# Copying x of the last two attention steps out of each PSUM bank with one ScalarE operation of 512 columns in place of two of 256

## The chip, the cores and the metric

The kernel runs on one core of a Trainium2 chip. The core's engines work side by side and each takes its own instructions in order: TensorE (PE for its matmuls, PEld for its weight loads), VectorE (DVE), ScalarE (ACT), GpSimd (POOL) and SyncE (SP), which issues most DMAs. Matmuls write into PSUM, eight banks of 512 f32 columns in 128 partitions; the other engines copy results from there to the on-chip memory SBUF. The metric is the device time of one execution in microseconds (us), the median of the runs shown.

## What is computed

A linear attention with decay, followed by a two-layer network with a tanh gelu. There are 4 batches, 8 heads, 768 positions, head width 64; the network goes from 512 to 2048 and back to 512 columns for 3072 tokens.

```python
for b in range(nb):                       # blocks of 64 positions
    intra = (q_b @ k_b^T * Dmask) @ v_b   # within the block, lam ** distance below the diagonal
    inter = (q_b * lam_pow) @ kv_state    # from all earlier blocks
    out[b] = intra + inter
    kv_state = lam**64 * kv_state + (k_b * rev_pow)^T @ v_b
x = out as 3072 tokens x 512              # 8 heads side by side
h = x @ w_in                              # 512 -> 2048
g = 0.5 * h * (1 + tanh(c * (h + 0.044715 * h**3)))
return g @ w_out                          # 2048 -> 512
```

## The kernel before

**Attention by steps.** The attention runs in 24 steps. A step is 256 positions of one batch (a "super-block", numbered 0 to 11) and one half of the heads, so steps 2n and 2n + 1 make up super-block n. For a step, q and k are scaled, cast and transposed; `scores` multiplies k with q into two banks S; `causal` (L360) multiplies the scores with the mask into PT on VectorE; PT and v give the part of x within the chunks of 128 positions (L460), and the running state u with q gives the rest (L498, or L488 for some steps, called narrow, whose second chunk lands in the other half of the partitions). Both are summed in PSUM in the two banks O0 and O1, one for each chunk of 128 positions; a step takes 256 columns of each bank. The state is advanced by `update` (VectorE L547 and L550, GpSimd L558 and L565).

**Two steps at once.** `burst(ns, ss, ...)` runs the scores of the steps `ns` and finishes x of two steps `ss`, which fill the two halves of both banks. It then makes the masked scores of `ns` (`causal`), copies x out of the banks, queues the network's work for the finished group of super-blocks, and advances the states of `ns`. Five bursts come before the last call, `burst((), (22, 23), 3, 4)`: here no scores are left to make, so `ns` is empty, and 22 and 23 are not narrow.

**Copying x.** `x_out(ss, O, swapped)` copies x of the steps in `ss` from the banks to the f16 tile xT of the group: for each of the banks c = 0, 1 one ScalarE operation (L529), or for the second bank of narrow steps two operations of 64 partitions each (L527). Each pair of neighbouring output columns comes from two places 64 columns apart in the bank, so the copy writes f16 values with a stride of two. For narrow steps, the two steps of a burst are given to `x_out` together (512 columns per operation); for other steps, one after the other (256 columns per operation). Four operations thus run in the last burst, in this order: step 22 from O0, step 22 from O1, step 23 from O0, step 23 from O1.

**The network by groups.** The network works on groups of super-blocks; the last group, number 6, holds super-blocks 10 and 11, that is steps 20 to 23. For groups 5 and 6 the first product, x times w_in, is made by a scheme of seven block products in place of eight (`seven`, matmuls at L796 into banks HX, HY and HW). It needs sums and differences of quarters of x, made by `sum_x` on VectorE (L775, tile xs). The quarters are numbered (C, T): C is the half of the columns (the head half), T the super-block within the group:

```python
X_SUMS = {1: ((0, 1), ALU.subtract, (0, 0)), 2: ((1, 1), ALU.subtract, 1),
          3: ((1, 1), ALU.subtract, (0, 1)), 4: ((1, 0), ALU.subtract, 2)}
```

So the first sum reads the quarter (0, 1), which is step 22, and the second reads the first sum and the quarter (1, 1), step 23. The block products of a set come in the order 1, 5, 2, 6, 3, 7, 4, where 4 falls into the next set. Product 1 (into HX) reads the quarter (0, 0) alone, which is step 20; product 5 (into HY) reads the first sum; product 2 (into HW) reads the quarter (1, 0); product 6 (HX) reads the second sum; product 3 (HY) reads the quarter (1, 1). ScalarE copies HX (L808, tile m) and HY (L808, tile q) for later additions on VectorE (L818), and writes the gelu (L814). The second layer is made by seven products too (`product`, matmuls at L692 into banks MX, MY and MW, copies at L714, additions at L734, L740 and L743).

**What sets the order.** The order of every engine's instructions is written out by hand: each one is pinned in program order. The network's pieces stand in a list `filler`, and calls of `fill(n)` between the attention's steps take n pieces from it. After the last burst, `fill(len(filler))` takes all that are left: first the rest of group 5's second layer, with group 6's products between them. The first piece taken after the last burst is a product MY of group 5, and the four `sum_x` of group 6 are issued behind it; on VectorE they stand behind an addition of group 5 (L734) that was issued before. SyncE's and GpSimd's queues hold nothing between the last states (L565) and the output's stores and an addition (L749) of group 5.

The profile names lines of the kernel: L498 matmuls that finish x, L529 the copies, L775 the sums of x, L796 the first layer's products of groups 5 and 6, L692 the second layer's.

Of the kernel before, what the change touches and what calls it, by code (L numbers as in the profile page):

```python
# [15 lines left out]
def kernel(  # L16
# [322 lines left out]
    def half64(i):  # L339
        return slice(64 * i, 64 * i + 64)  # L340
# [3 lines left out]
    def scores(n):  # L344
        o = qkT[n]
        Sps = [ps_M.tile([P, 2, 2, P], FP32, tag="M", name=f"S{hl}") for hl in range(2)]
        for hp in range(2):
            for jk in range(2):
                for hl, c in TILES:
                    pin(nc.tensor.matmul(  # L350
                        Sps[hl][half64(c), hp, jk, :], o[half64(hl), 1, jk, hp, half64(c)],
                        o[half64(hl), 0, :, hp, half64(c)], start=True, stop=True,
                        skip_group_check=True))
        Ss[n] = Sps

    def causal(n):

        t = ptp.tile([P, 2, 2, 2, P], FP16, tag="PT", name=f"PT_{n}")
        for hl, Sps in enumerate(Ss.pop(n)):
            pin(nc.vector.tensor_tensor(  # L360
                t[:, hl].rearrange("p b c d -> p b (c d)"), Sps[:].rearrange("p b c d -> p b (c d)"),
                mask[:].unsqueeze(1).to_broadcast([P, 2, 2 * P]), ALU.mult))
        PTs[n] = t
# [65 lines left out]
    def behind(ins):  # L429


        nop = nc.tensor.nop()
        tc.add_manual_dep(nop.ins, ins.ins.name, mybir.DependencyInfo(
            mybir.DependencyClass.Sync, mybir.DependencyReason.DATA))
        pin(nop)

    def burst(ns, ss, *mix, ahead=None):


        narrow = bool(NARROW & set(ss))  # L440
        for i, n in enumerate(ns):
            scores(n)
            if ahead and i == 0:
                ahead()
        O = [ps_M.tile([P, 2, 2, P], FP32, tag="M", name=f"O{c}") for c in range(2)]
        seen = set()

        def start(kind, c, hl):
            new = (kind, c, hl) not in seen
            seen.add((kind, c, hl))  # L450
            return new

        qTs = [qkT.pop(s) for s in ss]
        for i, s in enumerate(ss):
            PT, tv = PTs.pop(s), a16.pop(s)[2]
            for hp in range(2):
                for jk in range(2):
                    for c, hl in TILES:
                        to = hl ^ narrow * c
                        mm = nc.tensor.matmul(  # L460
                            O[c][half64(to), i, hp, :], tv[half64(c), jk, 2 * hp + hl, :],
                            PT[half64(c), hl, hp, jk, :], start=start("O", c, to), stop=False,
                            skip_group_check=True)
                        pin(mm)
        if ns:
            K = [ps_M.tile([P, 2, P], FP32, tag="M", name=f"K{c}") for c in range(2)]
        for i, n in enumerate(ns):
            _, tk, tv = a16[n]
            last = (n // 2) % NSB == NSB - 1
            for jk in range(2):  # L470
                for hp in range(2):
                    for c, hl in TILES:
                        if c == 1 and last:
                            continue
                        pin(nc.tensor.matmul(
                            K[c][half64(hl), i, hp * D : hp * D + D],
                            tk[half64(c), jk, 2 * hp + hl, :], tv[half64(c), jk, 2 * hp + hl, :],
                            start=start("K", c, hl), stop=(jk == 1), skip_group_check=True))
            Kps[n] = [t[:, i] for t in K]
        if narrow:  # L480
            behind(mm)
        for i, s in enumerate(ss) if narrow else ():
            u = [us.pop(key, None) for key in ((s - 2, 1), (s, 0))]
            for hp in range(2):
                for c, hl in TILES:
                    if u[c] is None:
                        continue
                    pin(nc.tensor.matmul(  # L488
                        O[c][half64(hl ^ c), i, hp, :], u[c][half64(hl), hp, :],
                        qTs[i][half64(hl), 0, :, hp, half64(c)], start=False, stop=True,  # L490
                        skip_group_check=True))
        for i, s in enumerate(ss) if not narrow else ():
            for c in range(2):
                if c == 0 and (s // 2) % NSB == 0:
                    continue
                u = us.pop((s, 0) if c else (s - 2, 1))
                for hp in range(2):
                    pin(nc.tensor.matmul(O[c][:, i, hp, :], u[:, hp].rearrange("p l d -> p (l d)"),  # L498
                                         qTs[i][:, 0, :, hp, half64(c)], start=False, stop=True,
                                         skip_group_check=True))  # L500
        for n in ns:
            causal(n)
        for batch in ((ss,) if narrow else [(s,) for s in ss]):
            i = ss.index(batch[0])
            x_out(batch, [t[:, i : i + len(batch)].rearrange("p i h t -> p (i h t)") for t in O],
                  swapped=narrow)
        sbg = ss[-1] // 2
        g, i = group_of[sbg]
        if ss[-1] % 2 == 1 and i == len(groups[g]) - 1:
            queue_group(g, *mix)  # L510
        for n in ns:
            update(n, 0)

    def x_out(ss, O, swapped=False):

        sbg, half = divmod(ss[0], 2)
        g, i = group_of[sbg]
        if g not in xT:
            xT[g] = xtp.tile([P, len(groups[g]), 2, 2, SB], FP16, tag="xT", name=f"xT_{g}")
        r = 4 * i + 2 * half  # L520
        dst = xT[g].rearrange("p b a h t -> p (b a h) t")[:, r : r + 2 * len(ss)]
        for c in range(2):
            d = dst[:, :, c * P : (c + 1) * P].rearrange("p r (t j) -> p r j t", j=2)
            o = O[c].rearrange("p (r j t) -> p r j t", j=2, t=D)
            if c == 1 and swapped:
                for hl in range(2):
                    pin(nc.scalar.activation(out=d[half64(hl)], in_=o[half64(1 - hl)], func=AF.Copy))  # L527
            else:
                pin(nc.scalar.activation(out=d, in_=o, func=AF.Copy))  # L529
# [5 lines left out]
    def update(s, c, parts="tu"):  # L535


        sbg, half = divmod(s, 2)
        sb = sbg % NSB
        if c == 1 and sb == NSB - 1:  # L540
            Kps.pop(s)
            return
        if "t" in parts:
            K = (Kps[s] if c == 0 else Kps.pop(s))[c].rearrange("p (hp d) -> p hp d", hp=2)
            t = ucp.tile([P, 2, D], FP32, tag=f"t{half}", name=f"t_{s}_{c}")
            if sb == 0 and c == 0:
                pin(nc.vector.tensor_copy(out=t[:], in_=K))  # L547
            else:
                for hp in range(2):
                    pin(nc.vector.scalar_tensor_tensor(  # L550
                        t[:, hp, :], state[half][:, hp, :],
                        lamu[:, 2 * half + hp : 2 * half + hp + 1], K[:, hp, :],
                        ALU.mult, ALU.add))
            state[half] = t
        if "u" in parts:
            if (s if c == 0 else s + 2) in NARROW:
                u = ubp.tile([P, 2, 2, D], FP16, tag=f"u{half}", name=f"u_{s}_{c}")[:, 0]
                pin(nc.gpsimd.tensor_tensor(  # L558
                    u, state[half][:],
                    lamu[:, 2 * half : 2 * half + 2].unsqueeze(2).to_broadcast([P, 2, D]),  # L560
                    ALU.mult))
                us[(s, c)] = u
                return
            u = ubp.tile([P, 2, 2, D], FP16, tag=f"u{half}", name=f"u_{s}_{c}")
            pin(nc.gpsimd.tensor_tensor(  # L565
                u[:], state[half][:].unsqueeze(2).to_broadcast([P, 2, 2, D]),
                lumask[:, 2 * half : 2 * half + 2, :].unsqueeze(3).to_broadcast([P, 2, 2, D]),
                ALU.mult))
            us[(s, c)] = u
# [566 lines left out]
    scale_v(16)  # L1136
    fill(3)
    burst((13, 14), (12,))
    fill(1)
    U(13)  # L1140
# [30 lines left out]
    fill(3)  # L1171

    burst((18, 19), (16, 17))
    prep_v(21)
    fill(2)
# [49 lines left out]
```

## Time and profile before

| | |
|---|---|
| median of 3 runs | 198.75 us (198.57 to 198.77) |
| the profiled execution's own time | 198.57 us |
| its span, first to last instruction | 196.8 us |
| granted TensorE clock, mean | 0.997 |
| TensorE matmul busy | 189.8 us, 96% of the span |
| VectorE busy | 145.8 us, 74% |
| ScalarE busy | 126.0 us, 64% |
| copies of x from O (L529) | 13: 10 of 128x256, 3 of 128x512 |
| last burst's copies | 159.52 to 160.91 us |
| last instruction of the chain | ScalarE copy L714, 192.95 to 193.33 us |

A line of the profile has the start and the length in us, the engine, the source line, the operation, the tiles (written<-read), the size of the operands (partitions x elements, type) and the number of such operations run together; behind it, in brackets, the idle time of the engine before it and what ended it. In the groups the last columns are the busy time and the mean length in ns. The chain of work that ended last is followed back from the last instruction: at each step to what released it, or to the instruction before it on its engine. Times are counted from the start of the span.

### The profile page before, as it was taken

Reading aid. Unit: us, or ns where it says so; the run is one execution under the profiler, and the core shown is the slowest. Engines: PE = TensorE matmul, PEld = TensorE weight load, DVE = VectorE, ACT = ScalarE, POOL = GpSimd, SP = SyncE. Lnnn points to the kernel's source line nnn. Section 1 sums busy time; section 2 is a strip of 40 time slices with the busy share of each in tenths; the row PEclk is TensorE's granted clock in tenths of the full one; section 3 lists DMA queues with packets and bytes.
Section 4 is the critical chain, followed back from the end, with each engine's and each line's share of the span. In section 5 each row is a group of like instructions: output and inputs, shape, how many; then the busy total and the mean of one; then the engine's idle time right before and its main releaser. Section 6 shows DMA issues by size and latency. Waiting matters only on the chain.

```text
span 196.8 us, 5996 instructions
## 1 busy us (share of the span) xinstructions
PE 189.8 (96%) x2467; PEld 138.7 (70%) x2469; DVE 145.8 (74%) x291; ACT 126.0 (64%) x250; POOL 68.9 (35%) x85
## 2 busy tenths in 40 slices
PE   8879999999999999999999999999999999999992
PEld 2546544456888888654688754588888888888881
DVE  4987722889999789959989836999557995478530
ACT  3673878357874796686846479835778856678211
POOL 6594213456445524438434506064002030002000
PEclk9999999999999999999999999999999999999998
DMA  5999999999999999999989999910630300021114
GB/s 171 291 324 384 388 384 389 299 289 291 242 217 218 250 215 238 240 176 267 331 253 236 269 344 154 152 27 0 47 113 3 110 5 0 3 107 67 43 61 154
DMA packets 62811, 38.13 MB, mean 194 GB/s; under 512 B 18624, under 2 KB 55744, under 8 KB 62784
## 3 DMA queue, kind: packets, MB, share of 16 engines
q1 hardware_dynamic: 62240, 37.50, 78.8%
q8 instruction: 19, 0.31, 0.7%
q10 hardware_dynamic: 544, 0.26, 0.5%
q14 instruction: 8, 0.07, 0.1%
HBM read 27.26 MB, written 6.29 MB: 171 GB/s over the span
## 4 chain that ended last, share of the span: by engine, by line
PE 89%; SPq 4%; DMA 4%; ACT 0%; issue 0%
PE Hps L613 25%; PE MX L692 18%; PE MY L692 9%; PE HX L796 7%; PE O2ps L628 7%; PE MW L692 4%; DMA wi<-in_moe_w_in_dram 4%; SPq L70 4%; PE HY L796 4%; PE S L350 3%; PE Hps L895 3%; PE HW L796 2%; PE O L460 1%; PE OK L400 1%; PE Tps L321 1%; PE OK L422 1%
## 5 line engine op out<-in xcount | busy, mean ns | idle before, releaser
L613 PE MATMUL Hps<-xT,w_in 128*128 128x512 f16 (+1 forms) x288 | 50.5, 332 | 0.0
L613 PEld LDWEIGHTS <-w_in 128*128 128x128 f16 x288 | 27.8, 98 | 19.4
L617 ACT ACTIVATE gT<-Hps 128x512 f16<-128x512 f32 x56 | 32.6, 597 | 9.0 <-PE Hps L613 8.5
L360 DVE TENSOR_TENSOR PT<-S,mask 128x512 f16<-128x512 f32 x48 | 30.4, 683 | 8.9 <-PE S L350 8.9
L266 POOL TENSOR_TENSOR v<-v,dv 128x512 f16<-128x512 f32 x24 | 27.7, 1156 | 19.4 <-DMA v<-in_v_dram 14.5
L692 PEld LDWEIGHTS <-gs 128*128 128x128 f16 x320 | 31.1, 98 | 3.7
L692 PEld LDWEIGHTS <-gT 128*128 128x128 f16 x240 | 23.2, 98 | 3.5 <-ACT gT L617 0.2
L565 POOL TENSOR_TENSOR u<-t,lumask 128x256 f16<-128x256 f32 x21 | 15.6, 757 | 21.1 <-DVE t L550 11.9
L692 PE MATMUL MX<-w_sum,gs 128*128 128x256 f16 x160 | 21.4, 273 | 0.0
L282 DVE TENSOR_TENSOR qk<-q,dq 128x512 f16<-128x512 f32 x23 | 19.0, 830 | 0.7 <-DMA q<-in_q_dram 0.5
L295 ACT ACTIVATE qk<-k 128x512 f16<-128x512 f32 x23 | 14.4, 625 | 7.8 <-DMA k<-in_k_dram 7.2
L749 POOL TENSOR_TENSOR o<-u,q 128x512 f32<-128x512 f32 (+1 forms) x5 | 6.0, 1197 | 37.2 <-issue 34.7
L662 DVE TENSOR_TENSOR gs<-gT 128x1024 f16<-128x1024 f16 (+1 forms) x24 | 16.1, 678 | 3.1 <-ACT gT L617 3.0
L558 POOL TENSOR_TENSOR u<-t,lamu 128x128 f16<-128x128 f32 x19 | 10.9, 582 | 19.7 <-DVE t L550 14.1
L628 PE MATMUL O2ps<-w_out,gT 128*128 128x512 f16 x64 | 14.6, 379 | 0.0
L796 PEld LDWEIGHTS <-ws 128*128 128x128 f16 x128 | 12.4, 98 | 1.6 <-DVE xs L775 0.2
L529 ACT ACTIVATE xT<-OK 128x256 f16<-128x256 f32 x22 | 8.7, 453 | 6.4 <-PE OK L413 3.1
L714 ACT ACTIVATE u<-MX 128x256 f32<-128x256 f32 x18 | 6.9, 384 | 7.4 <-PE MX L692 7.4
L628 PEld LDWEIGHTS <-gT 128*128 128x128 f16 x64 | 6.1, 98 | 6.6
L692 PE MATMUL MY<-w_out,gs 128*128 128x256 f16 x80 | 10.7, 273 | 0.0
L810 DVE COPY u<-HX 128x512 f32<-128x512 f32 x8 | 5.5, 690 | 6.8 <-ACT gT L814 4.4
L692 PE MATMUL MX<-w_sum,gT 128*128 128x256 f16 x80 | 10.4, 273 | 0.0
(105 smaller groups left out, 322.5 us busy)
## 6 DMA issues: line engine op xcount, KB each, us to landing
q<-in_q_dram SPq DMA_DIRECT2D x24, 256.0 KB, 5.2
k<-in_k_dram SPq DMA_DIRECT2D x24, 256.0 KB, 5.5
v<-in_v_dram SPq DMA_DIRECT2D x23, 256.0 KB, 5.4
out_dram<-o SPq DMA_DIRECT2D x23, 256.0 KB, 3.7
wo<-in_moe_w_out_dram SPq DMA_DIRECT2D x4, 1024.0 KB, 9.4
wi<-in_moe_w_in_dram SPq DMA_DIRECT2D x4, 512.0 KB, 7.2
wi<-in_moe_w_in_dram SPq DMA_DIRECT2D x2, 1024.0 KB, 12.6
v<-in_v_dram ACTq DMA_DIRECT2D x1, 256.0 KB, 4.2
```

The source lines that it names most:

```text
L266: pin(nc.gpsimd.tensor_tensor(wide(tv[:]), ld32[s][2][:], decay(dv, s), ALU.mult))
L282: pin(q_eng.tensor_tensor(wide(tq), q32[:], decay(dq, s), ALU.mult))
L295: pin(nc.scalar.activation(out=wide(tk), in_=k32[:], func=AF.Copy))
L360: pin(nc.vector.tensor_tensor(t[:, hl].rearrange("p b c d -> p b (c d)"), Sps[:].rearrange("p b c d -> p b (c d)"), mask[:].unsqueeze(1).t ...
L558: pin(nc.gpsimd.tensor_tensor(u, state[half][:], lamu[:, 2 * half : 2 * half + 2].unsqueeze(2).to_broadcast([P, 2, D]), ALU.mult))
L565: pin(nc.gpsimd.tensor_tensor(u[:], state[half][:].unsqueeze(2).to_broadcast([P, 2, 2, D]), lumask[:, 2 * half : 2 * half + 2, :].unsqueez ...
L613: pin(nc.tensor.matmul(by_block(Hps[:, i, :]), w_in16[:, c, f * P : (f + 1) * P], x(c), start=(c == 0), stop=(c == NC - 1)))
L617: pin(nc.scalar.activation(out=dst, in_=Hps[:], func=AF.Gelu_apprx_tanh))
L628: pin(nc.tensor.matmul(O2[tau][0][:], gT[:, f % HF, f // HF, tau * P : (tau + 1) * P], w_out16[:, f, :], start=(n == 0), stop=(n == NF - 1)))
L662: pin(nc.vector.tensor_tensor(g_rows(m, i), g_rows(a, i), g_rows(b, i), op))
L692: pin(nc.tensor.matmul(dst, lhsT, rhs, start=(opens and i == 0), stop=(closes and i == HF - 1), skip_group_check=True))
L796: pin(nc.tensor.matmul(dst[:, i, :], w_in_block(a, slice(c, c + 1), slice(f * P, f * P + P))[:, 0], x_block(b, slice(c, c + 1))[:, 0], sta ...
```

## The change

In `burst`, the two steps are given to `x_out` together also when the list `ns` is empty, which it is in the last burst alone. There, `x_out` then makes two ScalarE operations of 128 partitions by 512 columns, one for each bank and both steps, in place of four of 256 columns. The order becomes: steps 22 and 23 from O0, steps 22 and 23 from O1. The values written and where they are written are as before.

```diff
@@ burst @@
         for n in ns:
             causal(n)
-        for batch in ((ss,) if narrow else [(s,) for s in ss]):
+        for batch in ((ss,) if narrow or not ns else [(s,) for s in ss]):
             i = ss.index(batch[0])
             x_out(batch, [t[:, i : i + len(batch)].rearrange("p i h t -> p (i h t)") for t in O],
                   swapped=narrow)
```

## The prediction

> **What bounds the kernel now.** I read four views in this order: the page (engine shares and the chain that ended last), the chain piece by piece around the edited step, the timeline of all engines there, and narrow windows of the timeline on ScalarE for the price of one copy.
>
> The page first: line 1 has the engines, the other line the chain's shares.
>
> ```profile
> PE 189.8 (96%) x2467; PEld 138.7 (70%) x2469; DVE 145.8 (74%) x291; ACT 126.0 (64%) x250; POOL 68.9 (35%) x85
> ...
> PE 89%; SPq 4%; DMA 4%; ACT 0%; issue 0%
> ```
>
> TensorE (PE) carries 89% of the chain, ScalarE (ACT) rounds to 0%. So ScalarE's own time is worth nothing as such; only what it makes TensorE wait for is. Next, the chain around the last two steps (start, length, what):
>
> ```profile
> 158.47 0.57 PE O L460 x32
> 159.04 0.55 PE O L498 x8
> 159.59 1.31 PE MY L692 x12
> 160.90 0.44 PE HX L796 x4
> 161.34 0.50 PE HY L796 x4
> 161.84 0.44 PE MY L692 x4
> 162.28 0.44 PE HW L796 x4
> 162.71 0.44 PE HX L796 x4
> ```
>
> The x of steps 22 and 23 is finished in banks O0 and O1 by L498, then TensorE works without a break: 12 old products MY, a product HX, and HY. All pieces of four matmuls take 0.44 us, but this HY takes 0.50: 0.06 us is lost there. What it waits for is in the timeline (start, length, engine, line; in brackets the idle time before and what ended it):
>
> ```profile
> 158.97 0.62 PE L498 MATMUL O<-qkT,u 128*128 128x128 f16 x8
> ...
> 159.52 1.39 ACT L529 ACTIVATE xT<-O 128x256 f16<-128x256 f32 x4 [1.65 <-PE O L498]
> 159.56 0.68 DVE L662 TENSOR_TENSOR gs<-gT 128x1024 f16<-128x1024 f16 x1
> 160.16 0.68 DVE L734 TENSOR_TENSOR o<-MW,m 128x512 f32<-128x512 f32 x1
> ...
> 160.74 0.60 PE L796 MATMUL HX<-xT,w_in 128*128 128x256 f16 x4
> 160.76 0.41 DVE L775 TENSOR_TENSOR xs<-xT 128x512 f16<-128x512 f16 x1
> 161.22 0.33 PEld L796 LDWEIGHTS <-ws 128*128 128x128 f16 x4 [0.17 <-DVE xs L775]
> 161.23 0.61 PE L796 MATMUL HY<-xs,ws 128*128 128x256 f16 x4
> 161.28 0.42 DVE L775 TENSOR_TENSOR xs<-xT,xs 128x512 f16<-128x512 f16 x1
> ```
>
> This is the edited place. Four ScalarE copies run from 159.52 to 160.91. The first sum of x, on VectorE (DVE, xs at 160.76), reads xT of step 22: the copies of columns 0 and 1 of that step, the first two of the four. HY reads that sum: the sum ends at 161.17, the weight load for HY starts at 161.22. The wait is already exposed, so **any delay of that sum goes to TensorE one for one**, and TensorE carries the chain from there to the end.
>
> Why does the sum start at 160.76? Narrow windows show single copies (the first two rows here; the other rows are neighbours for the price of a larger copy):
>
> ```profile
> 159.52 0.46 ACT L529 ACTIVATE xT<-O 128x256 f16<-128x256 f32 x1 [1.65 <-PE O L498]
> 159.52 0.77 ACT L529 ACTIVATE xT<-O 128x256 f16<-128x256 f32 x2 [1.65 <-PE O L498]
> 126.28 0.76 ACT L529 ACTIVATE xT<-O 128x256 f16<-128x256 f32 x2
> 154.91 0.75 ACT L529 ACTIVATE xT<-O 128x512 f16<-128x512 f32 x1 [0.78 <-PE O L488]
> 155.69 1.50 ACT L527 ACTIVATE xT<-O 64x512 f16<-64x512 f32 x2
> ```
>
> The two copies of step 22 end at 159.52 + 0.77 = 160.29. The sum comes 0.47 us later: VectorE works in order and is in L734 (160.16 to 160.84), with the sum's start 0.08 inside its tail. So today the copies have about 0.42 us to spare (0.05 us of the 0.47 being the handover), and VectorE's queue decides.
>
> **The change, part by part.**
>
> *Removed and added.* Four copies of 128x256 (0.46 us each, about 0.31 apart) become two of 128x512: bank O0 for both steps, then bank O1 for both. Nothing moves in another queue; no DMA of SP or POOL is passed, and TensorE's and VectorE's orders stay.
>
> *Start of the first copy.* It now reads step 23's half of O0 too. L498's eight matmuls run 158.97 to 159.59, two per step and bank; the sixth, the last into O0, starts about 5 x 0.055 = 0.28 after the first (eight starts in 0.45 us of weight loads) and takes 0.22 (0.62 - 7 x 0.057): 159.47. Today's start at 159.52 is already 0.05 after that, although step 22's part of O0 was done about 159.25. So the bank as a whole was waited for before: **no change, 159.52**.
>
> *Length of a copy.* The same shape with the same pattern stands in the trace: 0.75 at 154.91 (x3, mean 749 ns in the groups). I take 0.75.
>
> *Distance of the two.* No pair of full 128x512 copies of this kind stands in the trace, so it is bounded. Below: pairs of 128x256 overlap by 0.46 + 0.46 - 0.77 = 0.15 (0.16 at 126.28), which would put the second 0.60 after the first; 0.58 if they overlap by 0.17. Above: at 154.91 the next copy starts 0.78 later, with no overlap, but that one moves 64 partitions to the other half. The 128x256 pairs are the nearer row (same line, same partitions), so I take 0.60 and keep 0.58 and 0.78.
>
> *Handover to VectorE.* VectorE's copy at 140.72 starts 0.06 after the ScalarE gelu that it waits for (140.03 + 0.63), the one at 177.66 0.07 after (176.96 + 0.63), and the sum at 71.40 0.03 after (70.77 + 0.60). I take 0.05, with bounds 0.03 and 0.07.
>
> *Sum.* The sum needs the second copy now (bank O1, step 22's half of it): 159.52 + 0.60 + 0.75 + 0.05 = **160.92** against 160.76, a delay of 0.16 us. Bounds: 159.52 + 0.58 + 0.75 + 0.03 = 160.88 (+0.12) and 159.52 + 0.78 + 0.75 + 0.07 = 161.12 (+0.36). The copies' spare 0.42 us is gone, and the wait changes from VectorE's own queue to ScalarE. Behind the waiting sum on VectorE stand the other three sums (161.28 to 162.37) and the add at 162.82; TensorE reads the second sum at 162.55, 0.85 after its end at 161.70, and both shift alike, so nothing adds. ScalarE's next work, the copy of HX at 161.37, waits for TensorE and lies after 160.87 (0.04 before today's last copy) or at worst 161.05: freeing ScalarE gives nothing. The banks are free in time too: no wait on them is seen before HX at 165.17.
>
> *Below nothing?* A gain would need HY earlier than now; at most the 0.06 it loses. VectorE's queue in front of the sum is untouched, so I exclude it: the low end is 0.
>
> *To the end.* From 161.34 the chain is TensorE without a gap, then the last copy at 192.95 and its store; the delay arrives whole. The profiled execution took 198.57 (span 196.8 and 1.8 around it) and would take 198.73. It is the fastest of the runs shown; on their median of 198.75 the forecast is **198.91 us**, +0.08%. A difference under 0.2% (0.40 us) is about what a measurement of this kernel cannot tell from no change, so my forecast counts as no change, on the slow side.
>
> *A rule of the Trainium skill against the change.* The row: ScalarE is 64% busy, and the bubble at HY is 0.06 us, today through VectorE. The page Perfetto Trace Analysis, section Optimizing Scalar/DVE Operations, holds that larger operations pay where the engine is saturated, and that where it is not, but makes other engines wait, breaking instructions up may let work finish sooner. By its first half the change would give the few hundredths of ScalarE time that nobody waits for, 198.75; by its second half it costs, as in the sum.
>
> *A rule that would make it free.* The page ScalarE: Activation LUTs, section What ACT_TABLE_LOAD costs, has an activation at 186 ns + 0.833 ns per column with an overlap of 93 ns; two of 512 would be estimated to end at 159.52 + 0.52 + 0.61 = 160.65, before VectorE is free, and the sum would be no delay. The plain 128x512 copies here (0.60) fit it; this pattern, at 0.75, does not, and the row decides.
>
> **The rivals.**
>
> 1. *Hidden.* The second copy ends by 160.71 and VectorE still decides: 198.75 to 198.80. For it: the sum today has 0.42 us of cover, and 128x512 copies in plain order take 0.60 (159.52 + 0.59 + 0.60 = 160.71). Against: all three of this pattern took about 0.75.
>
> 2. *Slower, by draining.* ScalarE does not overlap the two large copies. Place: between the copies of O0 and O1. Price: 159.52 + 0.78 + 0.75 + 0.05 = 161.10, +0.34: 199.09; up to +0.36 by the handover, and if the sum then takes the longest such row, 0.53 (at 128.17) instead of 0.41, +0.48: 199.23. It is over 0.2% once HY is 0.40 late, that is when the second copy ends after 161.11 with the sum at 0.41. For it: no 512-wide copy in the trace overlaps its successor (154.91, 155.69). Against: those successors change partitions, and the 64x256 copies, which do so too, do not overlap either, while the full 128x256 do.
>
> 3. *Not as described.* The new condition could catch other bursts. Only the last call has an empty list of next steps, so the program changes in this one place.
>
> **How the numbers follow.** Forecast (+0.12 to +0.20): 0.55. Hidden: 0.12. Draining: 0.23, of which 0.13 over +0.40 (the runs shown spread by 0.20 us). Something outside this neighbourhood that I don't see (a later wait with less slack, a shift of the early loads): 0.10, half of it slower and half faster by more than 0.2%. Slower: 0.13 + 0.05 + 0.03 from the forecast's upper end with that spread = 0.21. Faster: 0.05 + 0.01 from Hidden's lower end = 0.06. Within: 0.73. The range goes from 198.60 (Hidden, in a low median) to 199.23 (draining's end); the likeliest alone has 198.80 to 199.00.
>
> **What the changed profile would show.** In the groups, L529 from O: 128x512 x5 and 128x256 x6. At the place: two copies from 159.52, the second starting 0.60 later (0.78: rival 2) and ending near 160.87; the sum's wait named ScalarE and its start near 160.92 (still 160.76: rival 1); PEld before HY idle for 0.33 instead of 0.17; every later piece of the chain late by the same 0.16, the last copy at 193.11. The forecast is wrong if the copy is shorter than 0.6 here, if the first one starts later than 159.52, or if a later wait grows or shrinks so that the end does not move with HY.

## The result: 0.3% faster, and not at the place of the edit

The changed kernel takes 198.32 us, the median of 22 runs (198.10 to 199.08), against 198.81 us (198.57 to 200.22) for the kernel before, measured beside it: the ratio is 0.9969, with a 95% interval of 0.9957 to 0.9980 (the ratio is estimated from all runs and is not the quotient of the medians, 0.9975). The forecast was 198.91 and no change, with a range down to 198.60. So a gain came where a small loss was expected.

The page of the changed kernel has nearly the same shares of engines (busy us, share of the span, instructions) and of the chain, with two ScalarE instructions fewer:

```profile
span 196.5 us, 5993 instructions
PE 190.4 (97%) x2467; PEld 139.2 (71%) x2469; DVE 145.7 (74%) x291; ACT 125.7 (64%) x248; POOL 68.5 (35%) x85
...
PE 89%; SPq 4%; DMA 4%; ACT 0%; issue 0%
```

The timeline around the last burst (start, length, engine, line, operation; in brackets the idle time before and what ended it):

```profile
159.17 0.62 PE L498 MATMUL O<-qkT,u 128*128 128x128 f16 x8
...
159.72 1.34 ACT L529 ACTIVATE xT<-O 128x512 f16<-128x512 f32 x2 [1.65 <-PE O L498]
...
160.36 0.68 DVE L734 TENSOR_TENSOR o<-MW,m 128x512 f32<-128x512 f32 x1
160.94 0.60 PE L796 MATMUL HX<-xT,w_in 128*128 128x256 f16 x4
161.09 0.42 DVE L775 TENSOR_TENSOR xs<-xT 128x512 f16<-128x512 f16 x1
161.57 0.33 PEld L796 LDWEIGHTS <-ws 128*128 128x128 f16 x4 [0.31 <-DVE xs L775]
161.58 0.61 PE L796 MATMUL HY<-xs,ws 128*128 128x256 f16 x4
```

This execution is 0.20 us later than that of before when it gets here (L498 at 159.17 against 158.97), for reasons far ahead of the edit. Counted from L498, the copies start as before (0.55 after it), the first sum of x starts 1.92 after it instead of 1.79, and HY starts 2.41 after it instead of 2.26. **The local loss of 0.15 us is there, as forecast.** And it is carried to the end of the computation: the chain of the changed kernel ends with

```profile
189.76 3.51 PE MX L692 x32
193.27 0.02 issue
193.29 0.38 ACT o L714
```

where before the last ScalarE copy began at 192.95: later by 0.34, which is 0.20 + 0.15 within rounding. Yet the last store lands at 195.44 us instead of 195.70, and the span is 0.24 us shorter. Everything that is gained is gained after 193.7 us, in the last store of the output.

The DMA view shows it. First the kernel before, from just ahead of the issue of its last store to its landing (DMA: busy tenths in 40 slices of this window; GB/s per slice; the queues with packets, MB and share of the 16 DMA engines; then the stores issued in the window, with the KB and the us from issue to landing):

```profile
DMA  0699799979993027999953000000000000000000
GB/s 33 229 426 426 295 393 459 426 295 360 426 328 99 0 82 262 344 442 328 328 197 99 17 0 0 0 0 16 16 33 16 33 16 0 0 0 0 0 0 0
q1 hardware_dynamic: 288, 0.39, 44.2%
q14 instruction: 1, 0.01, 1.6%
out_dram<-o SPq DMA_DIRECT2D x1, 128.0 KB, 2.3
```

And the changed kernel, in the same place:

```profile
DMA  0849999596969999420468999997410000000000
GB/s 0 310 177 443 354 399 487 221 531 266 487 266 487 354 399 310 133 45 0 133 221 310 354 354 332 354 354 244 133 45 0 0 0 0 0 0 0 0 0 0
q1 hardware_dynamic: 288, 0.39, 59.5%
out_dram<-o SPq DMA_DIRECT2D x1, 128.0 KB, 1.7
```

In both, the first stretch of traffic is the store before it (256 KB) and the second is the last store. Before, the last store moves at 300 GB/s and more, falls to nothing for four slices, and then some packets trickle in at 16 to 33 GB/s: nearly all of the store has been moved and a small remainder is late. From 195 us on the view has nine packets:

```profile
DMA packets 9, 0.01 MB, mean 8 GB/s; under 512 B 1, under 2 KB 9, under 8 KB 9
```

By the DMA records these are eight packets of 1 KB and one of 4 bytes, one after the other, out of the store's 128 of 1 KB: a sixteenth, as one of 16 DMA engines would carry if the store were spread evenly over them (the records do not name the engine). In the whole window of the kernel before there is one packet on queue q14, which carries instructions; by the DMA records it is 8192 bytes, starts at 194.39 and takes 0.65 us, and the trickle begins at 195.04, when it ends. In the changed kernel there is no such packet beside the store, no trickle, and the store lands after 1.73 us instead of 2.34. The fetch of instructions comes at 197.15 there, after everything.

The sum is then 0.15 lost at HY and 0.61 saved at the last store, -0.46 us; the medians differ by -0.49, the lowest runs by -0.47, and the interval of the ratio stands for -0.40 to -0.85.

### The profile page after: what moved, and what is told of

The parts are those of the page before. It is cut to its first block, busy times and chain, and to the rows that moved or that the text cites. A ratio compares the mean times of both kernels' runs of the same rounds, so it can differ in the third digit from the quotient of the medians.

```text
span 196.5 us, 5993 instructions
## 1 busy us (share of the span) xinstructions
PE 190.4 (97%) x2467; PEld 139.2 (71%) x2469; DVE 145.7 (74%) x291; ACT 125.7 (64%) x248; POOL 68.5 (35%) x85
## 4 chain that ended last, share of the span: by engine, by line
PE 89%; SPq 4%; DMA 4%; ACT 0%; issue 0%
PE Hps L613 25%; PE MX L692 18%; PE MY L692 9%; PE HX L796 7%; PE O2ps L628 7%; PE MW L692 4%; DMA wi<-in_moe_w_in_dram 4%; SPq L70 4%; PE HY L796 4%; PE S L350 3%; PE Hps L895 3%; PE HW L796 2%; PE O L460 1%; PE OK L400 1%; PE Tps L321 1%; PE OK L422 1%
## 5 line engine op out<-in xcount | busy, mean ns | idle before, releaser
L282 DVE TENSOR_TENSOR qk<-q,dq 128x512 f16<-128x512 f32 x23 | 17.9, 780 | 1.1 <-DMA q<-in_q_dram 1.1
L350 PEld LDWEIGHTS <-qkT 64*64 64x64 f16 x384 | 6.3, 106 | 5.8 <-issue 2.8
```

The lines of the kernel that those rows point to most:

```text
L282: pin(q_eng.tensor_tensor(wide(tq), q32[:], decay(dq, s), ALU.mult))
L350: pin(nc.tensor.matmul(Sps[hl][half64(c), hp, jk, :], o[half64(hl), 1, jk, hp, half64(c)], o[half64(hl), 0, :, hp, half64(c)], start=True, ...
```

## The experiments

**Theory A:** ScalarE's instructions are fetched in blocks by DMA, and the request is tied to a place in its queue of instructions. Before, it came just behind the last copy and its fetch stood in front of a part of the last store. Two instructions fewer put the request behind the end of the stores. **Theory B:** the gain comes from the larger copies themselves. A third possibility, that fewer instructions are worth time as such, is tested along with these.

The idle instruction in several kernels is one more copy of an activation that is there already, one column wide and read by nobody, near the start:

```diff
     pin(nc.scalar.activation(out=warm[:], in_=ident[:, 0:1], func=AF.Gelu_apprx_tanh))
+    for _ in range(2):
+        pin(nc.scalar.activation(out=warm[:], in_=ident[:, 0:1], func=AF.Gelu_apprx_tanh))
```

It moves the line numbers behind it by two.

### The changed kernel with two idle instructions

The edit is the one shown, on the changed kernel.

> Changed kernel with two idle ScalarE activations of one column more at the start, so that ScalarE issues as many instructions as before. Theory A (the gain is an instruction fetch of ScalarE's queue that no longer falls beside the last store): the fetch is back near 194.7 us, the last store takes 2.3 us again, and only the delay of the first sum of x is left: +0.15 us on the kernel before (some 198.95 against 198.80). Theory B (the gain comes from the larger copies themselves): the time stays 0.5 us under the kernel before, 198.3.

Measured: 198.97 us (198.78 to 200.45), ratio 1.0006 (0.9987 to 1.0024) to a kernel before that had 198.92 on this chip. The gain is gone. The DMA view around its last store has everything back, packet, gap and trickle (by the DMA records the packet runs from 194.71 to 195.36, and the trickle begins at 195.35):

```profile
GB/s 0 252 410 378 347 378 441 410 315 378 410 252 63 0 142 299 315 488 299 284 158 32 0 0 0 0 16 16 32 16 32 16 0 0 0 0 0 0 0 0
q14 instruction: 1, 0.01, 1.5%
out_dram<-o SPq DMA_DIRECT2D x1, 128.0 KB, 2.4
```

and the timeline keeps the local delay: the first sum at 161.06, 1.92 after L498 (L500 here) at 159.14, and HY at 161.54, 2.40 after it. Theory B falls: the copies are the changed kernel's, and nothing is gained.

### The same merge in another burst

```diff
-        for batch in ((ss,) if narrow else [(s,) for s in ss]):
+        for batch in ((ss,) if narrow or ns == (20, 21) else [(s,) for s in ss]):
```

> Kernel before with the two copies of 512 columns in the burst of steps 18 and 19 (next steps 20 and 21) in place of the last burst: two ScalarE instructions fewer, and nothing edited in the last burst. Theory A: no fetch beside the last store, which lands in 1.7 us; no delay of the first sum of x of the last group: 0.61 us faster than before, 198.2, and 0.15 faster than the changed kernel. Theory B: as before, 198.8, with the fetch's place of no account.

Measured: 198.82 us (198.00 to 199.59), ratio 0.9985 (0.9965 to 1.0005): by the times alone undecided, with a median above the 198.2 that theory A had forecast. The profile decides the mechanism: no instruction packet beside the last store, which lands in 1.7 us, and HY 2.25 after L498, as in the kernel before:

```profile
q1 hardware_dynamic: 288, 0.39, 58.2%
out_dram<-o SPq DMA_DIRECT2D x1, 128.0 KB, 1.7
```

It also shows why the times spread. In the profiled execution, of 199.14 us, about a microsecond was lost at 94 us, where the scores waited for a transposed tile of q and k (the waits between 88 and 106 us):

```profile
PEld L350 <- DMA qkT<-qk: 1.0, 1, 1.0
```

Of its twelve runs, four took 198.00 to 198.11 and eight 198.79 to 199.59. That single runs divide there by this wait fits, but only the profiled one shows it.

### More instructions instead of fewer

Eight idle instructions on the kernel before.

> Kernel before with eight idle ScalarE activations of one column more at the start. Theory A: the same fetch is asked for eight instructions earlier, some 182 to 188 us, and is done before the last stores: the last store lands in 1.7 us, 0.6 us faster than before, 198.2, though ScalarE has more to do. Theory B: not faster, 198.8 or more. A theory that fewer instructions as such are worth time: slower.

Measured: 198.69 us (198.09 to 199.65), ratio 0.9985 (0.9966 to 1.0004), again undecided by the times alone and above the forecast 198.2, and again with a microsecond lost near 94 us in the profiled execution. The last store takes 1.8 us, and the instruction packet stands alone, at 188.27 by the DMA records. In the window from 188.2 to 188.7 us it is the only traffic:

```profile
q14 instruction: 1, 0.01, 3.8%
```

By the profiles, then, it is not the number of instructions that counts but where the fetch falls: eight more free the last store as well as two fewer.

### One idle instruction

> Changed kernel with one idle ScalarE activation more. Theory A: the fetch is asked for by the instruction that stands at one place of the queue; if that was the drain behind the last copy before, it is now the wait behind it at 196.0, the fetch falls after the stores and the time is the changed kernel's, 198.3. If it was the last copy itself, the fetch is at 194.7 and the time 198.95. Either way time and fetch go together. Theory B: 198.3 whatever the fetch does.

Measured, on the changed kernel: 198.55 us (198.19 to 199.61), ratio 0.9984 (0.9963 to 1.0006), so undecided by the times alone; the profiled execution took 198.30. The fetch comes at 196.81, behind the stores, and the last one lands in 1.75 us. With one instruction fewer than the kernel before, the request is already late enough; it was therefore tied to the drain, the instruction behind the last copy in ScalarE's queue (192.95 to 193.37 before), about 1 us ahead of the fetch. The traces bear this out in all ten profiles, those further below included: the late fetch starts 0.86 to 1.25 us after the end of the 319th ScalarE instruction on record, waits and drains counted, whichever instruction that is. In the kernel before it is that drain, in this one the wait behind it (at 195.79), and with two idle instructions on the kernel before the last copy but one.

### Both merges and the idle instructions again, on one chip

> The changed kernel again, for comparison on one chip with the next two. Theory A: some 0.45 us faster than before (0.61 saved at the last store, 0.15 lost at the first sum of x): a ratio near 0.9977.

> The kernel with the merged copies in the burst of steps 18 and 19 again. Theory A: 0.6 us faster than before (ratio near 0.997) and 0.15 faster than the changed kernel, where the shared rise at the q and k transposes near 94 us, which some runs have, falls alike on all. If merging there costs something of its own, its profile shows a longer chain between 125 and 130 us.

> The changed kernel with two idle ScalarE activations again. Theory A: 0.15 us slower than before (ratio near 1.0008), with the fetch at 194.7 us. Theory B: 0.45 faster, as the changed kernel.

The kernel before had 199.11 us here.

| kernel | median us (lowest to highest) | ratio (95%) | last store, us | HY after L498, us |
|---|---|---|---|---|
| changed kernel | 198.29 (198.09 to 199.35) | 0.9947 (0.9923 to 0.9971) | 1.75 | 2.40 |
| merge in the burst of steps 18 and 19 | 198.12 (197.95 to 199.47) | 0.9965 (0.9942 to 0.9989) | 1.75 | 2.25 |
| changed kernel, two idle instructions | 199.04 (198.83 to 199.97) | 1.0000 (0.9982 to 1.0018) | landing not recorded; 3.51 from issue to the span's end (2.84 in the first profile of the changed kernel) | 2.40 |

The first two are faster than before, the third is not: the same division as by the place of the fetch, which stood at 194.60 in the third and at 197.73 and 196.95 in the others. The first ratio is lower than the 0.9977 that the account gives, and its interval ends at 0.9971: here the kernel before was itself some 0.3 us slower than in the first measurement, for a reason that no run shows. The merge in the other burst costs nothing where it stands: the chain there has the same pieces, 0.57, 0.45, 0.28, 0.33 and 2.59 us, as before. In these runs it has the lowest median and the lowest single run (197.95), 0.17 below the changed kernel in the median, as the 0.15 at HY would give; but the intervals of the two ratios overlap, so that this last step isn't shown by the times.

### The fetch on the store before the last

Two idle instructions on the kernel before.

> Kernel before with two idle ScalarE activations more: one look at where the fetch falls. Theory A: it is asked for two instructions earlier, at the last copy but one (192.1 to 192.5 us), so it runs near 193.3 to 193.9, beside the last store but one; that one takes longer than 2.0 us, and the last store, which follows on the same engines, loses less than the 0.6 it loses before.

Measured in a single execution: 198.13 us. The fetch stands at 193.41, and the damage has moved with it: the view from 192 to 196.2 us has the last store but one (256 KB) at 2.3 us, where it took 2.03 before, and the last store at 1.8 (1.84, against 1.73 to 1.76 in the kernels with no fetch near it):

```profile
q14 instruction: 1, 0.01, 0.5%
out_dram<-o SPq DMA_DIRECT2D x2, 128.0 KB, 1.8
out_dram<-o SPq DMA_DIRECT2D x1, 256.0 KB, 2.3
```

(The x2 counts a second 128 KB store, whose issue reaches into that window and whose landing is not recorded.) With the store but one late, the last store takes 0.1 us longer here; a late last store delays the end by the whole 0.6. With this run, the same kernel with -2, -1, +2 and +8 ScalarE instructions is free of all but 0.1 us of the loss at the end, and with +0 it has it, whether the zero comes from the original copies or from merged copies and two idle instructions.

## Why the prediction was wrong

- **That the first sum of x would wait for the second copy** was right, in size too. The copies took 0.75 us, the second began 0.61 after the first (159.72 to 160.33; forecast 0.60), and the sum, counted from L498, was 0.13 later (forecast 0.16); HY was 0.15 later. VectorE's queue no longer decides: the sum starts at 161.09, 0.03 after the second copy ends (161.06), though the profile names no wait there, since L734 ends only at 161.04 (before, the sum started 0.08 ahead of that end).
- **That the bank as a whole was waited for before** was right: the copies start 0.55 after L498 in both kernels.
- **The two rules.** That breaking up instructions can help where an engine is not saturated but makes others wait (the Trainium skill, Perfetto Trace Analysis, section Optimizing Scalar/DVE Operations) is borne out at this place: 0.15 us. The price of an activation by which the change would have been free (the Trainium skill, ScalarE: Activation LUTs, section What ACT_TABLE_LOAD costs) is not: the copies took 0.75 us where it gives 0.61.
- **The step that failed is "To the end": "the delay arrives whole".** It does arrive at the last copy, but the forecast took the store behind that copy, and all that follows, as a constant, without a reason. The store was itself 0.61 us longer than it need be (2.34 against 1.73), and the change removed just that, which outweighs the 0.15 lost at HY. The store's 2.3 us stood in the list of DMA issues only as part of a group (two stores of 128 KB, median 2.0 us), and the packet that held it up was one of eight in the queue q14 of the page.
- **"ScalarE's own time is worth nothing as such"** is still right. What was overlooked is that a ScalarE instruction has a place in a queue that is fetched by DMA, so that removing it moves later fetches.
- **The part on other queues** ("no DMA of SP or POOL is passed") looked at the DMAs that the kernel issues and left out those that fetch its instructions.
- **The rivals:** draining did not occur (0.61 and not 0.78 apart), and Hidden did not either. What happened stood under "something outside this neighbourhood that I don't see", with 0.05 for the faster side and no mechanism.

The Trainium skill's page Runtime: NRT & Kernel Launch, section Instruction fetch mechanics, says that each engine's sequencer uses a DMA queue of its own to fetch the next block of instructions while it runs the current one. The runs here agree that the fetch runs beside the work and follows ScalarE's count of instructions. That the queue is ScalarE's own they do not show: with eight idle instructions on the kernel before, the packets of q14 at 48.74 and 194.39 move to 44.58 and 188.27, but those at 65.43, 116.02 and 159.88 are still at 65.63, 116.82 and 160.94. The page gives blocks of 16 KiB and calls the cost of crossing into the next one mostly hidden; here the packets of q14 have 8 KB, so that a packet need not be a whole block, and one of them was not hidden.

## What to carry to other kernels

When an edit adds or removes instructions, look at the tail separately from the place of the edit: what ends the kernel is the landing of the last store, and one instruction fetch beside it can be worth more than the edit itself. Compare the last store's time to landing with that of others of its size, and look in the DMA view of that window for a packet of an instruction queue; a few instructions more or less on that engine move it. A gain of this kind belongs to the program as a whole and not to the edit, and any later edit can undo it.

## What was not expected of the hardware

- An instruction fetch of 8 KB delayed the last store by 0.6 to 0.7 us (2.34 and 2.42 against 1.73 to 1.76), although the store's other packets were through: the late part moved at 16 to 33 GB/s and began when the fetch ended. The delay is about as long as the fetch itself, which took 0.65 and 0.64 us in these two; beside the store before the last it took 0.33 us, and that store was 0.3 us late. Alone it took 0.31 us (188.27 with eight idle instructions).
- Full 128x512 copies of this pattern overlap by 0.14 us (0.75 long, 0.61 apart in the changed kernel), while those that change partitions, or are followed by one that does, do not overlap at all (0.75 long, 0.78 apart in the kernel before).
